# The first unit of a fused attention and gated-FFN kernel: pair 0 on the hardware queue, key maxima from PSUM, masks laid a pair ahead

## The chip, the cores and the metric

The kernel runs on one core of one Trainium2 chip. The metric is the device time in microseconds. The time before is the median of three runs, 265.78 us (265.74 to 267.43).

## The reference

Sparse attention with a window and block summaries, followed by a gated FFN with a gated residual. Cut to what matters:

```
B, H, S, D = 4, 8, 768, 64;  block, window = 32, 16
k_sum = k.reshape(B, H, nb, block, D).max(axis=3)       # maxima of 32 keys, nb = 24
v_sum = v.reshape(B, H, nb, block, D).mean(axis=3)
scores_l = scale * q @ k.T,  masked where |i - j| >= window
scores_s = scale * q @ k_sum.T + log(block)
a = softmax(concat(scores_l, scores_s))                 # over keys and block maxima together
attn = a @ concat(v, v_sum)
x = attn, heads side by side                            # (3072, 512)
ffn = (gelu(x @ w_gate) * (x @ w_val)) @ w_out          # d_ff = 1536
out = x + sigmoid(x @ w_res) * ffn
```

## The kernel before

The 3072 rows are eight units of 384 tokens (half a batch of 768 each). A unit is attention for eight heads, taken as four pairs of heads, and then the FFN: 12 steps `fo` over d_ff, residual gate, output matmul. From unit 1 on, the attention of the next unit is woven into the end of the unit before. Unit 0 has nothing before it: its attention is the head of the program, written out by hand, and the order on each engine is the order of the program text.

All loads of k, q, v and the weights are software DMAs that GpSimd issues and that cast f32 to bf16 on the way. In the head GpSimd issues, in this order: k of heads 0 to 3, q of heads 0 to 3 (the first 384 tokens only, tile `qa`), k of heads 4 to 7, q of heads 4 to 7, chunks 0 to 6 of v (with the selects that build the mask `maskt`, the bias `bias_t` and the mean matrix `bmean` between them), then six slices each of `w_gate` and `w_val`, q's second half of batch 0 (`qb`), `w_res`, `w_out`, and in unit 0's step 4 the rows of batch 1. At most eight software DMAs are open at once: each waits for the one eight places before.

For each pair, `k_step` turns k with 16 TensorE transposes into one PSUM tile `tp`; ScalarE (ACT) copies it into `kW`, whose 128 columns for each 64-token tile hold the tile's own 64 keys, 16 on either side (the halo, copied from the neighbours) and 24 block maxima. `k_rest` builds the maxima on VectorE (DVE) from `kW` (L206, L208), copies the halos (L210, L211) and spreads the maxima to all 12 tiles (L212). `q_step` does the same for q with one ACT copy (L216). `mask_step` lays -30000 outside the window into the score tile by a matmul with `nmask` (L279); `s_step` adds the scores (L296), and ACT takes the exponential to `P` (L305, or L302 twice when the two heads lie in two tiles). The text of the head turns pairs 0 and 1 first, then scores pair 0, turns pair 2, scores pair 1, turns pair 3, scores pairs 2 and 3.

The values `vext` need two copies from their own loads (`v_spread`, L266, L269). `vsum_sum` (L254) makes the block means with seven matmuls, one a chunk of v. `av_part` multiplies P with the window's values and with the block means (L328), `av_norm` divides (L336, L338), and `xt_step` turns the result (L347). `keep_warm` issues matmuls of zeros. The first FFN matmuls are `gv` at L360. PSUM has four tiles `mm`, one `s` of double size, one `ao` and one `t`.

SP's queue carries only the outputs and, from unit 2 on, transposing DMAs.

Of the kernel before, what the change touches and what calls it, by code (L numbers as in the profile page):

```python
# [8 lines left out]
F32 = mybir.dt.float32  # L9
BF16 = mybir.dt.bfloat16  # L10
AF = mybir.ActivationFunctionType
ALU = mybir.AluOpType
# [3 lines left out]
def kernel(  # L16
# [11 lines left out]
    nc = tc.nc  # L28
    B, H, S, D = q.shape
    assert (B, H, S, D) == (4, 8, 768, 64)  # L30
    BLK, WIN = 32, 16
    NB = S // BLK
# [5 lines left out]
    FO = DFF // 128  # L38
    QT = 64
# [63 lines left out]
    with tc.manual_schedule():  # L103
# [17 lines left out]
        def mask_consts():  # L121
            nc.vector.memset(maskt[:], 1.0)
            select(maskt[0:96], ALU.is_ge, 0.0, -1, -1, 1)
            select(maskt[0:96], ALU.is_ge, 0.0, 2 * WIN - 1, 1, -1)
            nc.vector.tensor_scalar(nmask[:], maskt[:], 30000.0, -30000.0, ALU.mult, ALU.add)

# [4 lines left out]
        nc.vector.memset(bmean[:], 1.0 / BLK)  # L131
        vext_consts(0)

        kt, qa, qb = token_tile(0, S, "k0"), token_tile(0, TU, "qa"), token_tile(TU, S, "qb")
        k_sb[0] = kt
        load_tokens(kt, k, 0, 0, S, 0, 4)
        select(ident[:], ALU.not_equal, 1.0, 0, -1, 1)
        load_tokens(qa, q, 0, 0, TU, 0, 4)
        load_tokens(kt, k, 0, 0, S, 4, 8)
        load_tokens(qa, q, 0, 0, TU, 4, 8)  # L140
        select(bias_t[96:128, :], ALU.is_ge, -30000.0, NB - 1, 0, -1)
        load_values(0, 0)
        mask_consts()
        kw_consts(0)
        load_values(0, 1)
        select(bmean[:], ALU.is_ge, 0.0, 32 * (NB + 94) - WIN, -32, 1)
        select(bmean[:], ALU.is_ge, 0.0, 31 + WIN - 32 * (NB + 94), 32, -1)
        for c in range(2, NC + 1):
            load_values(0, c)
        nc.vector.memset(vsum[0][96:128, :, D:D + 1], 1.0)  # L150
# [3 lines left out]
        for c in range(6):  # L154
            sl = slice(c * 256, (c + 1) * 256)
            nc.gpsimd.dma_start(out=w_gate[:, :, sl], in_=wg_src[:, :, sl])
            nc.gpsimd.dma_start(out=w_val[:, :, sl], in_=wv_src[:, :, sl])
        load_tokens(qb, q, 0, TU, S, 0, H)
# [55 lines left out]
        def q_step(src, b, lo, hi, hp, pool, tag):  # L214
            tp = turn_pair(src, hp, pool, tag)
            nc.scalar.copy(qT[b % 2][hp][:, lo:hi].rearrange("d (p j) -> d p j", j=tp.shape[2]), tp)  # L216
# [59 lines left out]
        def mask_step():  # L276
            s = ps_s.tile([128, 2, 512], F32, tag="s", name="s")
            for hh in range(2):
                nc.tensor.matmul(s[:, hh, 0:TU].rearrange("p (t q) -> p t q", t=HT), ident[:],  # L279
                                 nmask.unsqueeze(1).to_broadcast([128, HT, QT]),  # L280
                                 start=True, stop=False, skip_group_check=True)
            return s

        def s_step(u, hp, st, s=None, two=None, masked=True):
            b, half = u // 2, u % 2
            first = s is not None
            if two:
                s = [pool.tile([128, 512], F32, tag=tag, name="s1") for pool, tag in two]
            elif not first:
                s = ps_s.tile([128, 2, 512], F32, tag="s", name="s")  # L290
# [120 lines left out]
        def values_step(u, fo):  # L411

            b = u // 2 + 1
            first = 8
            if u in (2, 4) and first - 3 <= fo < first + 1:
                block_sums(vT[b], fo - first + 3)
            if u in (1, 2, 4) and fo >= first:
                nb = 1 if u == 1 else b
                i = fo - first
                if i == 0 and u == 1:  # L420
                    vs = vsum_sum(nb, *SS)
                    vsum_out(nb, vs, 0, H, nc.scalar.copy)
                if i == 0:
                    v_spread(nb, 0, HT // 2, 0)
                if i == 2 and u > 1:
                    vsum_turn(nb, *SS)
                if i == 1:
                    v_spread(nb, 0, HT // 2, 1)
                if i in (2, 3):
                    vsum_bc(nb, 2 * i - 4, 0, HT)  # L430
                    vsum_bc(nb, 2 * i - 3, 0, HT)
# [9 lines left out]
        wp = ps_o.tile([128, 512], F32, tag="ao", name="wp")  # L441
        keep_warm(13, wp)
        nc.scalar.activation(pre[:], bias_t[0:1, :], AF.Exp)
        for hp in range(2):
            k_step(0, hp, *MM)
            q_step(qa, 0, 0, TU, hp, *MM)
        s = mask_step()
        keep_warm(3, wp)
        s_step(0, 0, st, s)
        k_step(0, 2, *MM)  # L450
        q_step(qa, 0, 0, TU, 2, *MM)
        s = mask_step()
        s_step(0, 1, st, s)
        k_step(0, 3, *MM)
        q_step(qa, 0, 0, TU, 3, *MM)
        s = mask_step()
        s_step(0, 2, st, s)
        v_spread(0, 0, HT // 2, 0)
        v_spread(0, 0, HT // 2, 1)
        vs = vsum_sum(0, *MM, range(0, 3))  # L460
        keep_warm(2, wp)
        s = mask_step()
        s_step(0, 3, st, s)
        keep_warm(2, wp)
        for c in range(3, NC + 1):
            vsum_sum(0, *MM, range(c, c + 1), vs)
            keep_warm(2 if c < NC else 1, wp)
        vsum_out(0, vs, 0, 2, nc.vector.tensor_copy)
        vsum_out(0, vs, 2, 8, nc.scalar.copy)
        nc.scalar.activation(pre[:], bias_t[0:1, :], AF.Gelu)  # L470
        homes = (AO, TT, MM, MM)
        for p in (0, 2):
            for hp in (p, p + 1):
                av_part(0, hp, st, *homes[hp], blocks=False)
            for hp in (p, p + 1):
                av_part(0, hp, st, blocks=True)
                av_norm(hp, st)
        keep_warm(3)
# [7 lines left out]
        for u in range(NU):  # L486
# [9 lines left out]
            for fo in range(FO):  # L496
# [29 lines left out]
                if u == 0 and fo >= FO - 2:  # L526
                    for hp in range(2 * (fo - FO + 2), 2 * (fo - FO + 2) + 2):
                        q_step(qb, 0, TU, S, hp, *(TT if hp % 2 else AO))
# [95 lines left out]
```

The softmax here doesn't subtract the row's maximum and nothing guards it: scores larger than these inputs give would overflow.

## Time and profile before

| what | value |
|---|---|
| median of three runs | 265.78 us |
| profiled execution, its own time | 265.32 us |
| its span | 263.4 us |
| TensorE busy | 254.6 us, 97% of the span |
| VectorE, ScalarE, GpSimd busy | 174.0, 139.0, 93.5 us |
| granted TensorE clock | 1.00 in every stretch |
| first FFN matmul (gv) starts | 22.78 us |

The span runs from the first to the last instruction of the profiled execution; 1.9 us of its own time lie around it. Shares of busy time are averages over stages that differ: the first 25 us are a chain of loads, turns, scores and values, and the rest is a steady stream of matmuls. A line "L360" is line 360 of the kernel.

### The profile page before, as it was taken

Reading aid. Unit: us, or ns where it says so; the run is one execution under the profiler, and the core shown is the slowest. Engines: PE = TensorE matmul, PEld = TensorE weight load, DVE = VectorE, ACT = ScalarE, POOL = GpSimd, SP = SyncE. Lnnn points to the kernel's source line nnn. Section 1 sums busy time; section 2 is a strip of 40 time slices with the busy share of each in tenths; the row PEclk is TensorE's granted clock in tenths of the full one; section 3 lists DMA queues with packets and bytes.
Section 4 is the critical chain, followed back from the end, with each engine's and each line's share of the span. In section 5 each row is a group of like instructions: output and inputs, shape, how many; then the busy total and the mean of one; then the engine's idle time right before and its main releaser. Section 6 shows DMA issues by size and latency. Waiting matters only on the chain.

```text
span 263.4 us, 5865 instructions
## 1 busy us (share of the span) xinstructions
PE 254.6 (97%) x2324; PEld 143.9 (55%) x2324; DVE 174.0 (66%) x414; ACT 139.0 (53%) x240; POOL 93.5 (36%) x124
## 2 busy tenths in 40 slices
PE   6799999999999999999999999999999999999994
PEld 2546555566555555555545565556555665556543
DVE  3744863498476889877837899678738853574424
ACT  2845449657565536754365536653375537553310
POOL 7976533997999107998300000000000000000000
PEclk9999999999999999999999999999999999999999
DMA  5999999999999979999991466224001200020012
GB/s 82 171 172 197 197 206 189 147 177 176 118 117 127 201 126 110 158 173 181 144 48 44 115 119 103 46 82 100 2 1 42 80 0 2 36 86 1 2 40 80
DMA packets 109259, 27.64 MB, mean 105 GB/s; under 512 B 95408, under 2 KB 106288, under 8 KB 109232
## 3 DMA queue, kind: packets, MB, share of 16 engines
q0 software_dynamic: 86032, 16.26, 83.2%
q1 hardware_dynamic: 23200, 11.02, 18.0%
q8 instruction: 18, 0.29, 0.5%
q14 instruction: 9, 0.07, 0.1%
HBM read 32.51 MB, written 6.29 MB: 147 GB/s over the span
## 4 chain that ended last, share of the span: by engine, by line
PE 89%; POOL 3%; DMA 3%; DVE 2%; issue 1%; ACT 1%; POOLq 0%; DVEq 0%
PE f L394 24%; PE g L360 23%; PE vv L360 22%; PE r L378 8%; PE ao L328 4%; DMA vext<-in_v_dram 3%; PE s L296 2%; PE xp L347 2%; POOL vext L99 2%; PE tp L185 1%; PE vs L254 1%; DVE gvT L367 1%; PE gv L360 1%; PE wp L409 1%; POOL k L90 1%
## 5 line engine op out<-in xcount | busy, mean ns | idle before, releaser
L360 PE MATMUL g<-xT,w_gate 128*128 128x384 bf16 x380 | 77.8, 326 | 0.5 <-DVE gvT L367 0.5
L366 ACT ACTIVATE ge<-g 128x384 f32<-128x384 f32 x95 | 46.7, 492 | 59.5 <-PE g L360 30.3
L360 PE MATMUL vv<-xT,w_val 128*128 128x384 bf16 x380 | 77.8, 326 | 0.1
L367 DVE TENSOR_TENSOR gvT<-ge,vv 128x384 bf16<-128x384 f32 x95 | 51.9, 552 | 30.9 <-PE vv L360 27.6
L394 PE MATMUL f<-w_out,gvT 128*128 128x512 bf16 (+2 forms) x312 | 69.5, 363 | 0.0
L360 PEld LDWEIGHTS <-w_val 128*128 128x128 bf16 x384 | 37.5, 98 | 25.6 <-issue 1.0
L360 PEld LDWEIGHTS <-w_gate 128*128 128x128 bf16 x384 | 36.9, 98 | 25.1 <-issue 1.1
L394 PEld LDWEIGHTS <-gvT 128*128 128x128 bf16 x312 | 27.6, 98 | 25.6
L349 ACT COPY xT<-xp 128x384 bf16<-128x384 bf16 x32 | 15.1, 481 | 22.6 <-PE xp L347 22.6
L378 PE MATMUL r<-w_res,xT 128*128 128x512 bf16 x96 | 24.4, 380 | 0.0
L399 DVE SCALAR_TENSOR_TENSOR th<-th,f 128x512 f32<-128x512 f32 (+2 forms) x26 | 16.7, 642 | 11.4 <-PE f L394 8.5
L172 POOL DMA_DIRECT2D k_sb<-in_k_dram x24 | 20.1, 864 | 11.6 <-DMA w_out<-in_moe_w_out_dram 5.2
L99 POOL DMA_DIRECT2D vext<-in_v_dram x28 | 23.2, 866 | 0.9 <-PE g L360 0.6
L384 ACT ACTIVATE th<-r 128x512 f32<-128x512 f32 x24 | 14.2, 602 | 17.4 <-PE r L378 17.4
L313 DVE TENSOR_TENSOR P<-P,maskt 128x768 bf16<-128x768 bf16 x28 | 15.5, 557 | 10.3 <-ACT P L305 7.5
L172 POOL DMA_DIRECT2D q_sb<-in_q_dram x24 | 19.9, 862 | 0.0
L338 DVE TENSOR_TENSOR xn<-ao,rz 128x384 bf16<-128x384 f32 x32 | 17.8, 558 | 1.1
L305 ACT ACTIVATE P<-s,bias_t 128x768 bf16<-128x768 f32 x18 | 16.2, 903 | 3.1 <-PE s L296 2.9
L336 DVE RECIPROCAL rz<-ao 128x6 f32<-128x6 f32 x32 | 6.1, 190 | 17.4 <-PE ao L328 17.4
L401 DVE SCALAR_TENSOR_TENSOR o<-th,xn 128x512 f32<-128x512 f32 (+2 forms) x26 | 16.9, 651 | 0.9
L302 ACT ACTIVATE P<-s,bias_t 128x384 bf16<-128x384 f32 x28 | 14.6, 578 | 0.0
L172 POOL DMA_DIRECT2D v_sb<-in_v_dram x16 | 13.5, 874 | 1.2 <-DMA q_sb<-in_q_dram 0.7
(82 smaller groups left out, 218.4 us busy)
## 6 DMA issues: line engine op xcount, KB each, us to landing
out_dram<-o SPq DMA_DIRECT2D x23, 256.0 KB, 2.6
vext<-in_v_dram POOLq DMA_DIRECT2D x20, 128.0 KB, 6.6
k_sb<-in_k_dram POOLq DMA_DIRECT2D x24, 96.0 KB, 6.1
q_sb<-in_q_dram POOLq DMA_DIRECT2D x24, 96.0 KB, 4.4
w_gate<-in_moe_w_gate_dram POOLq DMA_DIRECT2D x6, 256.0 KB, 8.6
w_val<-in_moe_w_val_dram POOLq DMA_DIRECT2D x6, 256.0 KB, 8.8
w_out<-in_moe_w_out_dram POOLq DMA_DIRECT2D x3, 512.0 KB, 14.1
v_sb<-in_v_dram POOLq DMA_DIRECT2D x16, 96.0 KB, 5.0
```

Of the source, the lines that this page charges most:

```text
L99: nc.gpsimd.dma_start(out=dst, in_=v[b, :, lo:hi, :].rearrange("h p d -> p h d"))
L172: nc.gpsimd.dma_start(out=sb[b][:, h // 2, :, h % 2 * D:h % 2 * D + D], in_=src[b, h].rearrange("(c p) d -> p c d", c=NC))
L305: nc.scalar.activation(P.rearrange("p a t q -> p a (t q)"), s[:, :, 0:TU], AF.Exp, scale=scale, bias=bias_t[:])
L313: nc.vector.tensor_mul(Pf, Pf, maskt.unsqueeze(1).to_broadcast([128, 2 * HT, QT]))
L338: nc.vector.tensor_mul(xn, ao[:, :, :, 0:D], rz.to_broadcast([128, NSUB, 2, D]))
L360: nc.tensor.matmul(acc[:, 0:TU], w[:, ko, fs], st["xT"][:, ko, :], start=(ko == 0), stop=(ko == KO - 1))
L366: nc.scalar.activation(ge[:], g[:, 0:TU], AF.Gelu)
L367: nc.vector.tensor_mul(gvT[:, fo, :], ge[:], vv[:, 0:TU])
L378: nc.tensor.matmul(r[:], st["xT"][:, ko, ss], w_res[:, ko, :], start=(ko == 0), stop=(ko == KO - 1))
L394: nc.tensor.matmul(st["f", sub][:, 0:c1 - c0], gvT[:, fo, ss], w_out[:, fo, c0:c1], start=(fo == 0), stop=(fo == FO - 1))
L399: nc.vector.scalar_tensor_tensor(th, th, 1.0, f[:, 0:c1 - c0], ALU.add, ALU.mult)
L401: nc.vector.scalar_tensor_tensor(o[:, 0:c1 - c0], th, 0.5, st["xn"][:, sub, c0:c1], ALU.mult, ALU.add)
```

## The change

Pair 0 of k and q goes by SP's hardware queue as f32 into two tiles `kf` and `qf`; ACT casts `kf` into `kt` and VectorE casts `qf` into `qa`. GpSimd loads the other three pairs one by one. `k_first` replaces `k_step` in the head: same transposes and ACT copy, but the maxima are one VectorE reduce straight from the PSUM tile, and halos and maxima are laid only for the six tiles of unit 0. The other six follow in `k_later`, at steps 4 to 7 of unit 0's FFN. In the head q's copy is VectorE's. Each pair's masks are laid before the scores of the pair ahead of it, for pairs 1 and 3 into `ao` and `t`. The turns of a pair now stand behind the scores of the pair before. There are 12 warming matmuls in place of 30. The block means are split between the scores and the value parts. q's second half is loaded before the last slice of the gate weights and turned at step 9, all four pairs together, in place of steps 10 and 11. In unit 1 the block means and the spreads of the next batch's values move from steps 8 and 9 to steps 9 and 10.

```diff
+        kw_consts(0)
+        nc.vector.memset(vsum[0][96:128, :, D:D + 1], 1.0)
...
-        load_tokens(kt, k, 0, 0, S, 0, 4)
+        kf = qk.tile([PP, 2, 8 * D], F32, tag="k_sb", name="kf")
+        qf = qk.tile([PP, 2, 4 * D], F32, tag="q_sb", name="qf")
+        nc.sync.dma_start(out=kf[:], in_=k[0, 0:2].rearrange("h (p j) d -> p h (j d)", j=8))
+        nc.sync.dma_start(out=qf[:], in_=q[0, 0:2, 0:TU].rearrange("h (p j) d -> p h (j d)", j=4))
+        load_tokens(kt, k, 0, 0, S, 2, 4)
         select(ident[:], ALU.not_equal, 1.0, 0, -1, 1)
-        load_tokens(qa, q, 0, 0, TU, 0, 4)
-        load_tokens(kt, k, 0, 0, S, 4, 8)
-        load_tokens(qa, q, 0, 0, TU, 4, 8)
+        load_tokens(qa, q, 0, 0, TU, 2, 4)
+        for h in (4, 6):
+            load_tokens(kt, k, 0, 0, S, h, h + 2)
+            load_tokens(qa, q, 0, 0, TU, h, h + 2)
+        load_values(0, 0)
+        select(maskt[0:96], ALU.is_ge, 0.0, -1, -1, 1)
+        select(maskt[0:96], ALU.is_ge, 0.0, 2 * WIN - 1, 1, -1)
         select(bias_t[96:128, :], ALU.is_ge, -30000.0, NB - 1, 0, -1)
-        load_values(0, 0)
-        mask_consts()
-        kw_consts(0)
-        load_values(0, 1)
+        for c in range(1, NC + 1):
+            load_values(0, c)
         select(bmean[:], ALU.is_ge, 0.0, 32 * (NB + 94) - WIN, -32, 1)
         select(bmean[:], ALU.is_ge, 0.0, 31 + WIN - 32 * (NB + 94), 32, -1)
-        for c in range(2, NC + 1):
-            load_values(0, c)
-        nc.vector.memset(vsum[0][96:128, :, D:D + 1], 1.0)
...
         for c in range(6):
             sl = slice(c * 256, (c + 1) * 256)
+            if c == 5:
+                load_tokens(qb, q, 0, TU, S, 0, H)
...
-        load_tokens(qb, q, 0, TU, S, 0, H)
...
-        def q_step(src, b, lo, hi, hp, pool, tag):
+        def q_step(src, b, lo, hi, hp, pool, tag, copy=nc.scalar.copy):
...
+        def k_first(hp):
+            tp = ps_mm.tile([128, 8, PP], BF16, tag="mm", name="tp")
+            for j in range(8):
+                for hh in range(2):
+                    nc.tensor.transpose(tp[hh * 64:hh * 64 + 64, j, :], kt[:, 2 * hp + hh, j, :], ident[0:PP, 0:PP])
+            kw = kW[0][hp]
+            nc.scalar.copy(kw[:, :, OWN:OWN + QT].rearrange("d t (p j) -> d t p j", j=8),
+                           tp.rearrange("d j (t p) -> d t p j", t=NT))
+            return tp, kw
+
+        def k_first_rest(tp, kw):
+            ks = work.tile([128, NB], BF16, tag="ks", name="ks")
+            nc.vector.tensor_reduce(out=ks[:], in_=tp.rearrange("d j (n w) -> d n j w", w=4),
+                                    axis=mybir.AxisListType.XY, op=ALU.max)
+            nc.vector.tensor_copy(kw[:, 0:HT, BLK0:BLK0 + NB], ks.unsqueeze(1).to_broadcast([128, HT, NB]))
+            nc.vector.tensor_copy(kw[:, 1:HT, 0:WIN], kw[:, 0:HT - 1, OWN + QT - WIN:OWN + QT])
+            nc.vector.tensor_copy(kw[:, 0:HT, POST:POST + WIN], kw[:, 1:HT + 1, OWN:OWN + WIN])
+
+        def k_later(kw):
+            nc.vector.tensor_copy(kw[:, HT:NT, 0:WIN], kw[:, HT - 1:NT - 1, OWN + QT - WIN:OWN + QT])
+            nc.vector.tensor_copy(kw[:, HT:NT - 1, POST:POST + WIN], kw[:, HT + 1:NT, OWN:OWN + WIN])
+            nc.vector.tensor_copy(kw[:, HT:NT, BLK0:BLK0 + NB], kw[:, 0:HT, BLK0:BLK0 + NB])
...
-            first = 8
+            first = 9 if u == 1 else 8
...
-        wp = ps_o.tile([128, 512], F32, tag="ao", name="wp")
-        keep_warm(13, wp)
         nc.scalar.activation(pre[:], bias_t[0:1, :], AF.Exp)
-        for hp in range(2):
-            k_step(0, hp, *MM)
-            q_step(qa, 0, 0, TU, hp, *MM)
-        s = mask_step()
-        keep_warm(3, wp)
-        s_step(0, 0, st, s)
-        k_step(0, 2, *MM)
-        q_step(qa, 0, 0, TU, 2, *MM)
-        s = mask_step()
-        s_step(0, 1, st, s)
...
+        keep_warm(8)
+        nc.scalar.copy(kt[:, 0:2].rearrange("p h j d -> p h (j d)"), kf[:])
+        nc.vector.tensor_copy(qa[:, 0:2].rearrange("p h j d -> p h (j d)"), qf[:])
+
+        def first_pair(hp):
+            t = k_first(hp)
+            q_step(qa, 0, 0, TU, hp, *MM, nc.vector.tensor_copy)
+            k_first_rest(*t)
+
+        first_pair(0)
+        nc.vector.tensor_scalar(nmask[:], maskt[:], 30000.0, -30000.0, ALU.mult, ALU.add)
+        keep_warm(1)
+        masked = [mask_step(), mask_step((AO, TT))]
+        s_step(0, 0, st, masked[0])
+        first_pair(1)
+        masked.append(mask_step())
+        keep_warm(1)
+        s_step(0, 1, st, masked[1], True)
+        first_pair(2)
+        masked.append(mask_step((AO, TT)))
+        keep_warm(1)
+        s_step(0, 2, st, masked[2])
+        first_pair(3)
+        keep_warm(1)
+        vs = vsum_sum(0, *SS, range(0, 2))
+        s_step(0, 3, st, masked[3], True)
+        nc.scalar.activation(pre[:], bias_t[0:1, :], AF.Gelu)
         v_spread(0, 0, HT // 2, 0)
         v_spread(0, 0, HT // 2, 1)
-        vs = vsum_sum(0, *MM, range(0, 3))
...
+        vsum_sum(0, *SS, range(2, 4), vs)
+        homes = (MM, MM, AO, TT)
+        for hp in range(2):
+            av_part(0, hp, st, *homes[hp], blocks=False)
+        vsum_sum(0, *SS, range(4, 5), vs)
+        for hp in range(2, NP):
+            av_part(0, hp, st, *homes[hp], blocks=False)
+        vsum_sum(0, *SS, range(5, NC + 1), vs)
         vsum_out(0, vs, 0, 2, nc.vector.tensor_copy)
         vsum_out(0, vs, 2, 8, nc.scalar.copy)
...
+        for hp in range(NP):
+            av_part(0, hp, st, blocks=True)
+            av_norm(hp, st)
-        keep_warm(3)
...
-                if u == 0 and fo >= FO - 2:
-                    for hp in range(2 * (fo - FO + 2), 2 * (fo - FO + 2) + 2):
+                if u == 0 and 4 <= fo < 8:
+                    k_later(kW[0][fo - 4])
+                if u == 0 and fo == FO - 3:
+                    for hp in range(NP):
                         q_step(qb, 0, TU, S, hp, *(TT if hp % 2 else AO))
```

## The prediction

> **What bounds the kernel now.** I read four views in this order: the page's engine row, the chain that ended last over the first 50 us, the timeline of the first 25 us, and the waits and DMA issues. The page says that TensorE is busy nearly throughout:
>
> ```profile
> PE 254.6 (97%) x2324; PEld 143.9 (55%) x2324; DVE 174.0 (66%) x414; ACT 139.0 (53%) x240; POOL 93.5 (36%) x124
> ```
>
> So from the first FFN matmul on, a microsecond is won or lost only where TensorE waits. The change touches the head, before that matmul, and two spots of unit 0's FFN loop. The chain over the head (start us, us, what):
>
> ```profile
> 10.25 7.42 DMA vext<-in_v_dram
> ...
> 17.71 0.38 PE vs L254
> ...
> 19.22 2.07 PE ao L328 x96
> ...
> 22.78 0.48 PE gv L360 x2
> ```
>
> The head ends when the first FFN matmul (gv) starts, at 22.78, and what ends last there is the load of v: its sixth chunk lands at 17.67, then come block means, attention times values, norms and transposes. The scores are not on this chain. The timeline shows how they run:
>
> ```profile
> 6.98 0.80 ACT L199 COPY kW<-tp 128x768 bf16<-128x768 bf16 x1 [4.67 <-PE tp L192]
> ...
> 7.81 0.36 DVE L206 TENSOR_TENSOR km<-kW 128x384 bf16<-128x384 bf16 x1 [0.46 <-ACT kW L199]
> ...
> 8.20 0.55 DVE L208 TENSOR_REDUCE ks<-km 128x24 bf16<-128x384 bf16 x1
> ...
> 8.90 0.60 DVE L212 COPY kW<-ks 128x288 bf16<-128x288 bf16 x1
> ...
> 10.10 0.90 ACT L305 ACTIVATE P<-s,bias_t 128x768 bf16<-128x768 f32 x1 [0.73 <-PE s L296]
> ...
> 10.49 0.22 DVE L212 COPY kW<-ks 128x288 bf16<-128x288 bf16 x1
> 10.90 0.79 ACT L199 COPY kW<-tp 128x768 bf16<-128x768 bf16 x1
> ...
> 15.79 0.90 ACT L305 ACTIVATE P<-s,bias_t 128x768 bf16<-128x768 f32 x1 [0.86 <-PE s L296]
> ```
>
> The exponentials P of pairs 0 and 3 start at 10.10 and 15.79: three pairs in 5.69, 1.90 each. That is possible because k and q of pairs 0 and 1 are both turned before the first P, so that while P of one pair runs, the next pair's key columns are already built.
>
> **Step 1, pair 0 arrives earlier.** Its k (384 KB as f32) and q (192 KB) go out on SP's queue, which is empty until the first output:
>
> ```profile
> out_dram<-o SPq DMA_DIRECT2D x23, 256.0 KB, 2.6
> ...
> out_dram<-o SPq DMA_DIRECT2D x1, 128.0 KB, 1.7
> ```
>
> No f32 load on this queue is in the trace. From below, 384 KB is the 2.6 of 256 KB plus 128 KB at the 394 KB/us at which f32 is read when the software queue is full (197 GB/s of bf16 in the windows): 2.9. From above it goes on with the step from 128 to 256 KB, 0.9 per 128 KB: 3.5. Issue at about 0.85 (ACT's first instruction stands at 0.81) gives 3.8 to 4.35; I take 4.0. [...]
>
> The new ACT cast of 96x1024: ACT copies of 384 and 768 columns take 0.48 and 0.80, so 0.83 ns a column and 0.16 fixed, 1.01: ends 5.06. Sixteen transposes, 0.53, end 5.63; kW copy 0.80, ends 6.47 (before: 7.78). VectorE's reduce of 768 from PSUM replaces a max (0.36) and a reduce of 384 (0.55): between 0.80 (ACT's pass over the same 768 columns) and 1.1 (twice the reduce); I take 0.95, near the 0.91 it replaces. The built program has it wait for ACT's kW copy, as these two readers of one PSUM tile were ordered before:
>
> ```profile
> ACT vsum L259 <- DVE vsum L259: 2.5, 1, 2.5
> ```
>
> So taking the maxima from PSUM saves nothing. Three smaller copies at the spacing of 0.12 seen before: 0.48, ends 7.93; nmask 0.1; four mask matmuls 0.66 (0.16 apart before), two more than before ahead of the first scores; scores 0.35, hand-overs 0.2: P of pair 0 at 9.2. Short VectorE copies are sometimes held while GpSimd builds descriptors (0.60 against 0.22 for the same L212 copy in the rows above); with 0.1 for that, **9.3**, bounds 8.4 (load 0.6 earlier, reduce 0.80, nothing held) to 10.0.
>
> **Step 2, what happens between the pairs.** This is what decides. In the changed program the order on ACT is kW0, P0, kW1, P1, kW2, P2, kW3, P3, and on TensorE the transposes of a pair stand behind the scores of the pair before. The look-ahead of one pair is gone: behind P of one pair wait kW of the next, then VectorE's maxima and copies, then TensorE's scores, then the next P. One round: P start to kW end 1.59 (10.10 to 10.90 + 0.79 in the rows), hand-over 0.03, reduce 0.95, copies 0.48, hand-over 0.15, scores 0.35, hand-over 0.06: 3.61. After pair 1, whose masks lie in two tiles and whose P is two instructions (two took 1.04 at 43.24), 3.74. q's copies, moved to VectorE, lie beside P and cost nothing; on ACT they would add 0.49 a round. The masks laid ahead also lie under P; behind it they would cost 0.5. Three rounds are 10.96; with 0.15 each for held VectorE copies 11.4 (bounds 10.5, with a reduce of 0.80 and nothing held, to 12.2). P of pair 3 starts at **20.7** instead of 15.79.
>
> **Step 3, from the last P to gv.** VectorE ends pair 3's key columns 0.56 before its P, then does both v_spread copies, 0.70 each (they stood at 15.15 and 15.88, under the wait for v): 21.6, and the first attention matmul waits for them. Four window parts at 0.27 and a chunk of block means 0.16, 22.85; the last two chunks 0.35; vsum to VectorE 0.30, 23.55; to ACT 0.47, 24.0; three block parts 0.8, 24.8; transpose and ACT's copy 0.7: gv at 25.55, or P + 4.85 (bounds 4.5 to 5.2). The three warming matmuls behind this stage (0.75 in the chain) are gone, which is counted here.
>
> Is v there? It is ahead of this. The software queue loses 288 KB of 1920, 1.5 us at its 190 KB/us. GpSimd issues six smaller loads for four ahead of v: +0.6 to +1.2; and the bmean selects (0.71) move behind v. The issues of v keep 0.88 each, the last full one near 10.6, landing (4.3 to 7.7 after issue in the batch-1 loads) at 15 to 18.3, under 21.6 all the same.
>
> So gv moves from 22.78 to **25.55, +2.8** (bounds +0.6: 8.4 + 10.5 + 4.5; +4.6: 10.0 + 12.2 + 5.2).
>
> **Step 4, unit 0's FFN.** The second half of the key columns (12 copies, 0.4 a pair at the spacing above) now stands in VectorE's queue at steps 4 to 7. At step 4 it follows the constants of batch 1, behind which TensorE already waited for a product at 34.65: +0.45 there (bounds 0 and 1.6, all four). From step 5 on VectorE has 0.56 + 0.4 of 1.30, covered. Turning q's second half at step 9 puts four pairs in a row on two tiles: the third waits for ACT's first copy, about 0.5 lost; in exchange the two waits of 0.4 to 0.5 at 40.3 to 41.2, where scores waited for these tiles, go: +0.1 (bounds -0.4 and +0.5). qb's load passes two of 256 KB, 2.6 us earlier than its 35.5, and slice 5 falls 2.0 behind while the queue is 1.5 ahead: it had landed at 33.6 for 36.6, so it costs nothing; uncovered 0.5. The moved value step of unit 1 leaves VectorE 0.75 behind at step 10; the scores and residual matmuls (some 4 us) before its product is needed hide it, else 0.75.
>
> **Sum:** +2.8 + 0.45 + 0.1 = +3.3. The profiled execution took 265.32 (span 263.4 and 1.9 around it), so 268.6; the median of the runs is 0.46 above that execution, so **269.0** against 265.78.
>
> **Rivals.**
> (a) *The same chain, but short.* k lands by 3.4, nothing holds VectorE, step 4 is hidden: +0.8 to +2.6, 266.6 to 268.4, within 1%. For it: most 0.22 copies were not held. Against it: GpSimd issues DMAs through the whole head.
> (b) *TensorE's clock falls.* The opening matmuls show a slow start: weight loads follow each other at 0.43, then five in 0.96; the granted clock reads 1.00 in both stretches, so that view will not tell.
>
> ```profile
> 3.80 0.15 PEld L409 LDWEIGHTS <-warm 128*128 128x128 bf16 x1 [0.28 <-issue]
> ...
> 4.17 0.96 PEld L409 LDWEIGHTS <-warm 128*128 128x128 bf16 x5 [0.22 <-issue]
> ```
>
> Before, TensorE never idles over 0.8 in the head; now it works some 1.7 of each 3.8, with about 2.1 idle in one piece and 18 of 30 warming matmuls gone. If it falls back, about 3 us of dense work on the way to gv and behind it take twice as long: +1.5 to +3, 270.5 to 272. [...]
> (c) *v still decides, and it is faster.* With v landed at 15.2 and gv 5.1 behind as now, less the 0.75 of warming, gv starts at 19.6: -3.2 + 0.5, 263.1. It begins to win when P of pair 3 starts before 17.9 (22.78 - 4.85), a round of 2.87 from 9.3. For it: v is the bound today and gets lighter. Against it: ACT alone holds 1.6 of each round, and reduce, copies and scores follow in a row.
> (d) *The maxima run beside ACT's copy after all.* 0.8 off each of three rounds and off pair 0: P of pair 3 at 17.5, gv at 22.35, 265.9. The built wait speaks against it.
>
> **How the numbers follow.** My forecast (268.4 to 270.5) 0.48; (a) 0.27; (b) 0.17; (c) 0.04; (d) 0.04. A measurement of this kernel can tell about 1%, 2.7 us. Slower by more than 1%: the forecast and (b), 0.65; within: (a) and (d), 0.31; faster: (c), 0.04. The range 266.8 to 271.4 takes in nearly all of (a) and half of (b), and leaves out some 0.17.
>
> **What would show it.** Right: P of pairs 0 to 3 some 3.7 apart, kW of a pair directly behind P of the one before; gv near 25.5; the chain through the head on ACT kW, DVE ks and kW, PE s, with no DMA of v. Wrong: starts of P less than 2.9 apart; the reduce starting before ACT's copy ends; gv before 22.8. Step 1 is wrong if the cast starts outside 3.4 to 4.6; step 4 if step 5's product does not come late; (b) shows in the spacing of the attention and first FFN matmuls.

## The result, and the profile after

The changed kernel took 275.56 us (median of 4 runs, 273.9 to 275.68) against 266.06 for the kernel before: a ratio of 1.033, 95% interval 1.028 to 1.039. It is slower by 9.5 us, where the forecast was 3.3. The profiled execution took 273.9, with a span of 272.2 against 263.4.

The page of the changed kernel, its engine row and its row of TensorE's granted clock (tenths of full speed in 40 slices of the span):

```profile
PE 256.0 (94%) x2282; PEld 145.4 (53%) x2306; DVE 176.8 (65%) x427; ACT 138.9 (51%) x239; POOL 94.3 (35%) x126
...
PEclk9765699999999999999999999999999999999999
```

TensorE is busy a little longer than before (256.0 against 254.6) with fewer instructions: some of them ran slower. The clock row, which was all nines before, falls in slices 2 to 5, about 7 to 34 us.

The timeline of the head (start us, us, engine, line):

```profile
6.76 0.96 DVE L232 TENSOR_REDUCE ks<-tp 128x24 bf16<-128x768 bf16 x1
...
8.32 1.28 PE L308 MATMUL s<-nmask,ident 128*128 128x384 bf16 x4 [1.94 <-DVE nmask L481]
...
10.14 0.90 ACT L334 ACTIVATE P<-s,bias_t 128x768 bf16<-128x768 f32 x1 [3.41 <-PE s L325]
10.94 0.79 ACT L226 COPY kW<-tp 128x768 bf16<-128x768 bf16 x1
...
13.72 1.05 ACT L331 ACTIVATE P<-s,bias_t 128x384 bf16<-128x384 f32 x2 [1.99 <-PE s L325]
...
17.55 0.90 ACT L334 ACTIVATE P<-s,bias_t 128x768 bf16<-128x768 f32 x1 [2.09 <-PE s L325]
...
21.21 1.05 ACT L331 ACTIVATE P<-s,bias_t 128x384 bf16<-128x384 f32 x2 [2.06 <-PE s L325]
...
28.58 0.50 PE L376 MATMUL xp<-ident,xn 128*128 128x128 bf16 x3 [1.10 <-DVE xn L367]
...
29.65 0.48 PE L389 MATMUL gv<-xT,w_gate 128*128 128x384 bf16 x1
```

The P's stand 3.58, 3.83 and 3.66 apart, each with kW of the next pair directly behind it; the chain that ended last runs over kf's load, ScalarE's kW copies, VectorE's reduces and copies and the scores, with no transfer of v. So far it is the chain of the forecast. Two things are not: masks that should take 0.66 took 1.28, and from P of pair 3 to the first FFN product gv it is 8.44 us instead of 4.85.

The stretches of 5 us show why (stretch, its length, then busy us and count of PE, PEld, DVE, ACT and POOL, granted clock, DMA share, GB/s):

```profile
5.00:10.00 5.00, 2.70 (x43) 1.41 (x45) 2.41 (x7) 1.10 (x2) 4.80 (x9) 0.85 1.46 172
10.00:15.00 5.00, 3.38 (x67) 2.34 (x66) 2.52 (x6) 2.87 (x5) 4.88 (x8) 0.81 2.20 134
15.00:20.00 5.00, 3.02 (x40) 1.64 (x39) 2.68 (x6) 2.05 (x3) 5.00 (x8) 0.53 1.31 164
20.00:25.00 5.00, 4.32 (x66) 2.28 (x65) 1.91 (x6) 2.54 (x4) 2.68 (x4) 0.50 1.41 187
25.00:30.00 5.00, 3.32 (x57) 2.34 (x57) 3.03 (x9) 1.14 (x3) 1.81 (x3) 0.50 1.45 197
30.00:35.00 5.00, 5.00 (x29) 2.86 (x28) 0.57 (x2) 2.28 (x6) 2.81 (x4) 0.76 1.42 199
```

In stretches of 1 us the clock is at half from 8.5 to 11.9, full again until 15.3, and at half from there to 32.4 us: in the whole stage behind the last P, and in the first 2.7 us of the FFN. The product of step 2 starts 8.2 us later than before (34.00 against 25.79), gv 6.9 later; the 1.3 between them is dense work at half rate (products 0.32 apart up to 32.17, 0.16 from 32.62 on). The span is 8.8 longer.

### The profile page after: what moved, and what is told of

Same layout as the page of the kernel before. It is cut to its first block, busy times and chain, and to the rows that moved or that the text cites. A ratio compares the mean times of both kernels' runs of the same rounds, so it can differ in the third digit from the quotient of the medians.

```text
span 272.2 us, 5827 instructions
## 1 busy us (share of the span) xinstructions
PE 256.0 (94%) x2282; PEld 145.4 (53%) x2306; DVE 176.8 (65%) x427; ACT 138.9 (51%) x239; POOL 94.3 (35%) x126
## 3 DMA queue, kind: packets, MB, share of 16 engines
HBM read 32.51 MB, written 6.29 MB: 143 GB/s over the span
## 4 chain that ended last, share of the span: by engine, by line
PE 85%; DVE 6%; DMA 4%; ACT 2%; issue 1%; DVEq 0%; ACTq 0%
PE f L423 23%; PE g L389 21%; PE vv L389 20%; PE r L407 8%; PE ao L357 3%; PE s L325 3%; DMA kW<-k_sb 3%; PE xp L376 2%; PE vs L280 2%; DVE ks L232 1%; DMA kf<-in_k_dram 1%; PE tp L186 1%; DVE xn L367 1%; ACT kW L226 1%; PE gv L389 1%
## 5 line engine op out<-in xcount | busy, mean ns | idle before, releaser
L423 PE MATMUL f<-w_out,gvT 128*128 128x512 bf16 (+2 forms) x298 | 68.6, 362 | 0.7
L407 PE MATMUL r<-w_res,xT 128*128 128x512 bf16 x88 | 23.6, 380 | 0.6 <-issue 0.3
L428 DVE SCALAR_TENSOR_TENSOR th<-th,f 128x512 f32<-128x512 f32 (+2 forms) x26 | 16.7, 641 | 11.4 <-PE f L423 8.5
L331 ACT ACTIVATE P<-s,bias_t 128x384 bf16<-128x384 f32 x32 | 16.7, 578 | 4.1 <-PE s L325 4.1
L334 ACT ACTIVATE P<-s,bias_t 128x768 bf16<-128x768 f32 x16 | 14.4, 901 | 7.1 <-PE s L325 7.0
L357 PEld LDWEIGHTS <-P 128*64 128x64 bf16 (+2 forms) x432 | 9.7, 120 | 8.2 <-issue 7.6
## 6 DMA issues: line engine op xcount, KB each, us to landing
out_dram<-o SPq DMA_DIRECT2D x23, 256.0 KB, 2.0
w_gate<-in_moe_w_gate_dram POOLq DMA_DIRECT2D x6, 256.0 KB, 8.6
w_val<-in_moe_w_val_dram POOLq DMA_DIRECT2D x6, 256.0 KB, 9.9
```

The source lines that it names most:

```text
L331: nc.scalar.activation(P[:, hh].rearrange("p t q -> p (t q)"), s[hh][:, 0:TU], AF.Exp, scale=scale, bias=bias_t[:])
L357: nc.tensor.matmul(ao[64 * e:64 * e + 64, sub, hh, :], P[rows, hh, t, :], rhs, start=blocks is None or (not blocks and sub == 0 and hh == ...
L407: nc.tensor.matmul(r[:], st["xT"][:, ko, ss], w_res[:, ko, :], start=(ko == 0), stop=(ko == KO - 1))
L423: nc.tensor.matmul(st["f", sub][:, 0:c1 - c0], gvT[:, fo, ss], w_out[:, fo, c0:c1], start=(fo == 0), stop=(fo == FO - 1))
L428: nc.vector.scalar_tensor_tensor(th, th, 1.0, f[:, 0:c1 - c0], ALU.add, ALU.mult)
```

## The experiments

Theory A: the clock takes the larger part of the loss, the lost look-ahead the rest. Theory B: the look-ahead is everything, the clock only a record. Theory C, added when the traces were compared: the first transposes of x wait for the wrong buffer. The diffs are against the changed kernel unless another is named.

### The clock: warming matmuls in the gaps (e1)

```diff
-        keep_warm(1)
+        keep_warm(8)
         masked = [mask_step(), mask_step((AO, TT))]
...
-        keep_warm(1)
+        keep_warm(7)
         s_step(0, 1, st, masked[1], True)
...
         homes = (MM, MM, AO, TT)
+        keep_warm(3)
...
             av_norm(hp, st)
+        keep_warm(3)
```

The gaps behind pairs 2 and 3 have seven as well.

> The changed kernel with warming matmuls of zeros (8, 7, 7 and 7, and 3 on either side of the value parts) in the gaps where TensorE waited; nothing else moved. Theory A (the clock gate took most of the loss, about 6 of 9 us, the lost look-ahead the rest): the granted clock stays at 1.00, the exponentials P of the four pairs still start about 3.6 apart, gv starts near 26 instead of 29.65, total 269 to 270. Rival B (the lost look-ahead is the whole cost, the slow clock only a record of the idling): gv stays near 29, total 274 to 276.

Measured: 272.24, ratio 1.022 (1.018 to 1.025), 3.3 less than the change, between the two theories; gv at 28.00 instead of 29.65. The clock was 1.00 from 5 to 25 us, but 0.51 in the next stretch:

```profile
25.00:30.00 5.00, 4.53 (x48) 2.65 (x43) 2.41 (x7) 1.17 (x3) 2.62 (x4) 0.51 1.45 197
```

So B's 274 to 276 is out, and A half shown: the clock fell again, and in the middle of work. These are 1-us stretches, and the block parts (P times the block means) in which it fell; the row's bracket is the longest idle time of TensorE from 21.63 to 25.04:

```profile
24.00:25.00 1.00, 0.64 (x29) 0.52 (x30) 0.50 (x3) 0.47 (x1) 0.42 (x2) 1.00 1.46 198
25.00:26.00 1.00, 0.72 (x31) 0.71 (x26) 0.97 (x3) 0.00 (x0) 0.44 (x2) 0.54 1.45 205
...
24.23 1.49 PE L357 MATMUL ao<-vsum,P 32*64 32x65 bf16 x48 [0.39 <-DVE vsum L285]
```

From 21.63 to 25.04 TensorE was busy for 2.89 of 3.41 us, with no transpose among it: attention matmuls of 65 columns, and 0.65 us of block means.

### The look-ahead back, without and with warming (e2, e3)

```diff
         masked = [mask_step(), mask_step((AO, TT))]
-        s_step(0, 0, st, masked[0])
         first_pair(1)
-        masked.append(mask_step())
+        s_step(0, 0, st, masked[0])
         keep_warm(1)
-        s_step(0, 1, st, masked[1], True)
         first_pair(2)
+        masked.append(mask_step())
+        s_step(0, 1, st, masked[1], True)
...
```

> The changed kernel with the turns of pairs 1, 2 and 3 put before the scores of the pair ahead again; the warming matmuls stay as in the changed kernel (one a pair). Theory A: P of pair 3 starts near 16 to 17 instead of 21.2, but the clock still falls in the gap ahead of the first masks near 8, so the values and the first FFN matmuls run at half clock: gv near 24, total 268 to 271. Rival B: gv near 21.5, total 264 to 266.

Measured: 269.96, ratio 1.015 (1.012 to 1.017). P's 11.42, 13.43, 15.21, 17.23: 1.9 apart, as before the change. Yet gv started only at 24.42, 7.2 behind the last P, with the clock at 0.75 from 20 to 25 us and 0.57 in the next stretch, and with a wait that has nothing to do with either:

```profile
23.36 0.50 PE L376 MATMUL xp<-ident,xn 128*128 128x128 bf16 x3 [1.38 <-DVE xn L367]
```

e3 adds 4, 2, 3, 3, 3 warming matmuls in the gaps and three each ahead of the value parts and of x's transposes.

> Both: turns a pair ahead and the gaps filled with warming matmuls. Theory A: clock 1.00 throughout, P of pair 3 near 16.5, then v (landed near 17.4) or the spreads decide, gv near 21.5 to 22.5: 264.5 to 266, level with the kernel before or a little faster. Rival B: no better than the run with the turns alone.

Measured: 268.46 (266.48 to 270.77, 10 runs), ratio 1.008 (1.005 to 1.012). Short of what A gives; the runs differ by over 4 us, which left something open (see e13 and e14).

### Does a slow clock alone cost time? (e4)

The kernel before, without the 17 warming matmuls that follow the first 13.

> The kernel before without the 17 warming matmuls behind the opening 13 (3, 2, 2, 7 and 3 taken out), nothing else. Theory A: the clock falls to 0.5 somewhere between 8 and 20 and the values and first FFN matmuls run at half rate: 268 to 272. Rival B (only one gap longer than the 2 to 3 us now seen can make the clock fall; the kernel before has none over 1.5): the clock stays at 1.00, and without the 0.75 of the last three it is 265 to 266.

Measured: 266.38, ratio 0.999 (0.996 to 1.002). Both theories' numbers missed. The clock did fall, from 11.5 to 18.3:

```profile
10.00:15.00 5.00, 3.84 (x71) 2.32 (x64) 2.47 (x9) 3.52 (x5) 4.42 (x7) 0.65 3.25 148
15.00:20.00 5.00, 5.00 (x71) 2.23 (x70) 2.97 (x8) 2.57 (x5) 3.28 (x6) 0.67 1.82 176
20.00:25.00 5.00, 4.52 (x97) 3.27 (x92) 2.73 (x8) 3.53 (x7) 3.25 (x5) 1.00 1.45 197
```

It was back before the last stage. P of pair 3 came at 18.30 instead of 15.79, and yet gv at 22.50 instead of 22.78, since 17 warming matmuls fewer stood on the way. The right comparison is e12 below, which leaves out only four of the same matmuls and keeps the clock: P of pair 3 at 16.22, gv at 22.11. So of the 2.1 us by which the slow clock held the last scores, 0.4 reached gv; most of the rest lay in the 2.8 us that e12 spends behind its last scores on block means and the warming between them. It was not free: in e4 the chain to gv runs over the slow matmuls,

```profile
3.86 7.89 DMA qa<-in_q_dram
...
15.80 1.39 PE vs L254 x3
...
18.26 1.13 PE vs L254 x4
```

and no longer over v's load.

### The buffers of the first transposes (e5), and with warming (e6)

```diff
-            xt_step(0, hp, st, *(TT if hp % 2 else AO), nc.scalar.copy)
+            xt_step(0, hp, st, *(MM if hp < 2 else TT if hp % 2 else AO), nc.scalar.copy)
```

The changed kernel gives the accumulators of pairs 2 and 3 the buffers `ao` and `t` (`homes = (MM, MM, AO, TT)`; before `(AO, TT, MM, MM)`), and the first transposes of x write to the same two: they wait until pairs 2 and 3 are normalised.

> The changed kernel with one edit: the first two transposes of x go into mm tiles, since the tiles ao and t now hold the value parts of pairs 2 and 3 and are free only after the third and fourth norm. Theory C (this wait, which the prediction did not have, is a term of its own): the first transposes start at the end of the block parts, 1.0 to 1.5 earlier than at 28.58, gv near 28.3, total 273.8 to 274.8. Rival: the norms pace the transposes anyway (0.70 a pair), so 275 to 276.

Measured: 273.98, ratio 1.029 (1.025 to 1.033): 1.6 less than the change. With four runs of each the intervals of the two ratios overlap, so the size is uncertain; that the wait is gone shows in the trace, where the transposes follow the block parts directly:

```profile
26.85 1.71 PE L357 MATMUL ao<-vsum,P 32*64 32x65 bf16 x48 [0.39 <-DVE vsum L285]
...
28.49 0.98 PE L376 MATMUL xp<-ident,xn 128*128 128x128 bf16 x6
```

gv came at 29.56 although this execution's last P, at 22.17, came a microsecond later than the change's: 7.39 behind it instead of 8.44.

e6 is e1 with this, and three more warming matmuls ahead of the block sums' copies.

> The first experiment (gaps filled with warming matmuls) with that edit and three more warming matmuls ahead of the block parts, so that the clock stays up to the FFN. Theory A and C together: the clock is 1.00 through the head, what is left is the lost look-ahead alone: P of pair 3 near 20.5, gv near 25.5, total 268.5 to 269.5, which is what the prediction made without the clock. Rival B: 271 or more.

Measured: 270.76, ratio 1.015 (1.010 to 1.021), between the two forecasts, clock 1.00 in every stretch. With e5 this prices the clock: 273.98 - 270.76 = 3.2, less what the warming itself costs. The two traces have it by place: P of pair 0 0.2 (11.18 against 10.99), three rounds 0.3 (10.99 against 10.70), last P to gv 1.1 (7.39 against 6.30), gv to the product of step 2 2.1 (5.09 against 3.01). That is 3.7 up to there; the two executions as a whole differ by 2.9.

### Warming only from the last gap on (e9)

e6 with one warming matmul in each of the first three gaps, as the changed kernel has.

> The kernel e6 (changed kernel, first two transposed tiles of x in other buffers, warming matmuls throughout) with only one warming matmul in each of the first three gaps, as the changed kernel has; the warming from pair 3's gap on stays (7, 3, 3, 3). Theory A': a round between two P is ScalarE and VectorE work (kW copy, reduce, copies), so a slow clock costs nothing there and all of its price is paid behind the last P; and without eight warming matmuls ahead of the first masks P of pair 0 comes earlier (10.1 to 11 instead of 11.0). Median 269.5 to 271, that is e6's 270.76 or a little less; the clock at 0.5 to 0.9 between 8 and 20 us and at 1.00 from 22 us on; three rounds 10.6 to 11.1. Rival: each round pays for its transposes, masks and scores at half rate, 0.5 a round and 0.3 at the opening: three rounds of 12.2 and a median of 272.3 or more.

Measured: 272.68, ratio 1.023 (1.019 to 1.028): worse than e6 by 1.9. The time is the rival's, the place is neither's:

```profile
19.14 3.17 PE L438 MATMUL wp<-warm 128*128 128x512 bf16 x7
...
22.85 0.35 PE L325 MATMUL s<-qT,kW 64*128 64x64 bf16 x12
```

The first two rounds were 3.80 and 3.98 (e6: 3.51 and 3.68), 0.3 each for the slow clock (0.77 from 10 to 15 us, 0.57 from 15 to 20); then the seven warming matmuls, themselves slow, held the scores of pair 3, whose key columns were complete at 21.14, and the last round took 5.08. From P to gv it was 6.29, as in e6. These seven began with the clock down and took 3.17; the same seven in e6, at 1.00, took 1.69.

### Look-ahead from pair 1 on (e8), and with late warming (e11)

e8 is e6 with pair 2 turned before the scores of pair 1 and pair 3 before those of pair 2.

> Both repairs and the tile edit on the changed kernel: pair 0 scored as soon as it is there, the turns of pairs 2 and 3 ahead of the scores of pairs 1 and 2, gaps filled. Theories A and C: clock 1.00, P of pairs 0 and 3 near 9.5 and 17, gv near 22, total 264.8 to 266; rival B: 267 or more.

Measured: 268.39, ratio 1.007 (1.005 to 1.010): 2.4 below e6, but in B's range and not in A's and C's. The clock was 1.00 in every stretch; what missed was P of pair 0, at 11.15 and not 9.5, behind eight warming matmuls that took 3.60. P of pair 3 at 19.43, gv at 25.72: again 6.29 behind.

e11 is e2 with e5's buffers, three warming matmuls ahead of the value parts and of the block sums' copies, and the second half of the key columns one step later.

> The changed kernel with the look-ahead back (turns of a pair ahead of the scores of the pair before, as in e2), the first two transposed tiles of x in other buffers, three warming matmuls ahead of the value parts and three ahead of the block sums, and the second half of the key columns at steps 5 to 8 instead of 4 to 7. By theory (look-ahead, clock behind the last P and the tile wait are the whole loss): P of pair 3 near 17.2 as in e2, gv 6.2 behind it at 23.4, the product of step 5 no later than the shift of the others: 265.8 to 267.2, ratio within 0.5% of the kernel before. Rival (the norms, v or the value copies hold the stage, as e3's gv at 25.55 with P at 18.32 suggests): gv at 24.5 or later and a median of 267.7 or more.

Measured: 268.91 (266.87 to 272.35, 12 runs), ratio 1.008 (1.005 to 1.011). The rival's number, but not its mechanism: without warming in the gaps the clock was 0.50 from 10 to 20 us in the profile, P of pair 3 came at 19.41, and gv 7.0 behind it.

### Maxima beside ScalarE's copy (e10)

e6 with k turned a second time into a tile of its own, from which VectorE takes the maxima ahead of q's copy. It makes rival (d) true.

> The kernel e6 with k of each pair transposed twice, into two tiles: ScalarE copies one, VectorE takes the maxima from the other at once, ahead of q's copy. This makes the fourth rival of the prediction true (the maxima run beside ScalarE's copy). If the round is the chain kW copy, reduce, copies, scores, as its steps have it: P start to reduce end about 1.3, q copy to 1.85, copies to 2.35, scores and hand-overs 0.5: rounds of 2.85 instead of 3.57, P of pair 3 2.1 to 2.5 earlier (19.2 to 19.6), gv at 25.5 to 26 and a median of 268.2 to 268.8 (e6: 270.76). If something else sets the end of the stage (v, the value copies), P comes earlier but gv stays near 28 and the median near 270.5. If the two passes over PSUM hold each other up, rounds stay above 3.3 and the median above 270.

Measured: 271.72, ratio 1.019 (1.016 to 1.023): no gain. Reduce and copy do run side by side, at 0.96 and 0.79 as in the changed kernel:

```profile
12.44 0.96 DVE L233 TENSOR_REDUCE ks<-t 128x24 bf16<-128x768 bf16 x1 [3.25 <-PE t L231]
...
12.50 0.79 ACT L226 COPY kW<-tp 128x768 bf16<-128x768 bf16 x1
```

But rounds shortened only to 3.30, 3.26 and 3.30: the reduce starts 0.74 behind P, when the second set of transposes is done, and q's copy then stands between it and the key columns. In the second and third round the scores also start 0.34 and 0.42 behind the finished key columns, behind e10's own warming and block means. The three rounds gained 0.8 together, and pair 0 lost 0.7 to the added transposes ahead of the warming.

### The opening, and everything undone but the loads (e13, e14)

Of the ten profiles with eight opening matmuls, up to e11, five turned pair 0's k in 0.53 us and five in 0.85. e13 is e6 with thirteen opening matmuls, and 4, 5, 5, 5 in the gaps. e14 is e3 with thirteen, e5's buffers, and three more ahead of the block sums' copies.

> The kernel e6 with thirteen opening warming matmuls, as the kernel before has, instead of eight, and 4, 5, 5, 5 in the gaps behind the four pairs instead of 8, 7, 7, 7. Of ten profiles with eight opening matmuls five turned pair 0's k at full rate (0.53 us) and five at half rate (0.85); in e6 it was half, and its eight warming matmuls then took 3.27 ahead of the masks, so P of pair 0 started at 10.99. Theory D (the cut opening is a cost of its own, and the rest of e6's loss is the lost look-ahead at full clock): transposes at 0.53 in the profile, P of pair 0 near 10.0, rounds of 3.55, P of pair 3 at 20.6 to 20.9, gv at 26.6 to 27.2, a median of 269.0 to 270.0 and a spread under 1.5. Rival (the opening doesn't matter, the two groups of e6's times come from elsewhere): P of pair 0 still at 10.8 or later and a median of 270.3 to 271.5.

> The kernel e3 (turns of a pair ahead of the scores of the pair before, warming in the gaps) with thirteen opening warming matmuls instead of eight, the first two transposed tiles of x in other buffers, and three warming matmuls ahead of the block sums: every part of the change that the runs found to cost time undone, and its loads, its maxima from PSUM, its order of the value parts and its moved steps kept. By theory D with the others: P of pair 0 at 10.8, P of pair 3 at 17 to 17.8, gv at 23.2 to 24, a median of 266.2 to 267.2. Rival (the stage behind the last P is itself 1.3 longer than before at any clock): gv at 24.3 or later and a median of 267.4 to 268.5.

Measured: e13 271.28, ratio 1.018 (1.016 to 1.021); e14 267.36, ratio 1.004 (1.002 to 1.007).

```profile
1.26 5.18 PE L438 MATMUL wp<-warm 128*128 128x512 bf16 x13 [1.26 <-DVE warm L121]
...
6.38 0.53 PE L224 MATMUL tp<-ident,k 96*64 96x96 bf16 x16
```

In e13 the transposes ran at full rate and the spread was 0.95, as theory D had it, but the median is the rival's: thirteen matmuls last until 6.4, and pair 0's k, cast by 5.37, waits for them. P of pair 0 started at 10.49, so the opening is a trade and no gain.

e14 landed just above D's 267.2, and less than 0.5% above the kernel before:

```profile
17.52 1.05 ACT L331 ACTIVATE P<-s,bias_t 128x384 bf16<-128x384 f32 x2 [0.96 <-PE s L325]
...
23.80 0.32 PE L389 MATMUL gv<-xT,w_gate 128*128 128x384 bf16 x1 [0.16 <-ACT xT L378]
```

e13 and e14 differ in the look-ahead alone (and a few warming matmuls): 271.28 - 267.36 = 3.9, and gv 27.82 against 23.80, 4.0.

### The hardware-queue load alone (e7), and a leaner kernel before (e12)

e7 is the kernel before with pair 0 of k and q by SP's queue and cast; nothing else.

> The kernel before with the hardware-queue load of pair 0 alone (kf, qf, the two casts, GpSimd's first two loads halved). If the load of v is the bound and the software queue gets 1.5 lighter: P of pair 0 near 9, v's sixth chunk near 16.3 instead of 17.67, gv near 21.5, total 264.3 to 265. Rival: v's landing is set by GpSimd's issue times, which do not move: gv at 22.5 or later, total 265.5 to 266.5.

Measured: 266.16, ratio 0.999 (0.997 to 1.002). P of pair 0 at 9.65 instead of 10.10, gv at 23.41 instead of 22.78 with the clock at 0.66 from 10 to 15 us, where the masks took 0.82 instead of 0.50; that is part of the delay. The chain to gv begins with the software queue's load of the other pairs' q, which lands at 10.98; pair 0 is not on it, so its 0.45 buys nothing here. What it is worth with the clock kept was not tried.

e12, against the kernel before, leaves out the last four warming matmuls:

```diff
-            keep_warm(2 if c < NC else 1, wp)
+            if c < NC:
+                keep_warm(2, wp)
...
-        keep_warm(3)
```

> The kernel before without the last four warming matmuls (one behind the last chunk of block means, three ahead of the first transposes of x): the first attention matmul no longer stands behind 0.37 of warming, nor the first transpose of x behind 0.75. If these matmuls stand on the chain that sets the end, as the chain of waits shows, gv starts 0.6 to 0.9 earlier than 22.78 and the median is 265.2 to 265.7. Rival 1 (the clock falls in the gaps left, the first product at half rate): 266.2 to 268. Rival 2 (norms of the second pair of pairs or the weights set the FFN's pace anyway): gv earlier, step 2's product where it was, 266.0 to 266.3.

Measured: 265.57 (12 runs), ratio 0.997 (0.995 to 0.999): faster than both kernels, as forecast, if by 0.3%.

```profile
21.20 0.52 PE L347 MATMUL xp<-ident,xn 128*128 128x128 bf16 x6
...
22.11 0.32 PE L360 MATMUL gv<-xT,w_gate 128*128 128x384 bf16 x1 [0.39 <-ACT xT L349]
```

gv started 0.67 earlier, and the clock stayed at 1.00, so these four warming matmuls were not needed to keep it. In the profiled execution (265.45) the 0.6 stands until 128 us, and a wait of 1.3 for a product of gvT in a later unit, 0.5 in the profile of before, takes it back; the medians have it.

## Why the prediction was right in direction and short by six microseconds

The direction and the chain through the head came out; the size did not. By the runs the 9.5 us are:

| part | from which runs | us |
|---|---|---|
| wait for the accumulators' buffers | 275.56 to 273.98 (e5) | 1.6 |
| slow clock, less the price of the warming | 273.98 to 270.76 (e6) | 3.2 |
| lost look-ahead | e13 to e14 | 3.9 |
| what stays | e14 over its 266.02 | 1.3 |

They add to 10.0; the half over 9.5 is e13's distance from e6, within the intervals.

**Step 1 held, with a price at the end.** kf landed at 4.23 (4.0 said), its cast took 1.04 (1.01), kW's copy ended at 6.73 (6.47), the reduce took 0.96 (0.95) and waited for ScalarE's copy as said. Then masks at half rate made 1.28 of 0.66, and P of pair 0 came at 10.14 (9.3, bound 10.0).

**Step 2 was right.** Three rounds took 11.07, forecast 11.4; P of pair 3 21.21, forecast 20.7: pair 0 was 0.8 late and the rounds 0.3 shorter. The time allowed for held VectorE copies, 0.1 and three times 0.15, did not show: the three copies of a pair took 0.49, 0.45, 0.38 and 0.38 (0.48 said before that allowance), beside GpSimd's issues, and no run shows that these issues are what makes a copy long. e14 against e13 shows that the lost look-ahead costs 3.9 when the clock is full. At full clock and with the buffers right, e6 took 270.76, 1.8 over the forecast and inside its range.

**Step 3 failed: P of pair 3 to gv, 4.85 forecast, 8.44 measured.** Three terms were missed.

- The clock, 1.1 of it, and 1.3 more in the FFN behind gv (2.1 in e5, whose clock recovered later: 0.60 from 30 to 35 us, against 0.76). The fall stood as rival (b), put at 1.5 to 3; e5 and e6 measure 3.2. The fault was the chance, 0.17: I took the longest gap, 2.1 by my sum and 1.94 in the trace, as the whole case, and that the clock would outlast it was not shown by the trace of before, where TensorE stands idle for at most 0.78 between two matmuls of the head. The stretches of 1 us show that the clock fell right behind that gap:

```profile
7.00:8.00 1.00, 0.00 (x0) 0.00 (x0) 0.96 (x4) 0.00 (x0) 0.88 (x2) 1.00 1.20 172
8.00:9.00 1.00, 0.68 (x3) 0.35 (x3) 0.27 (x4) 0.00 (x0) 1.00 (x2) 0.76 1.61 180
9.00:10.00 1.00, 1.00 (x16) 0.38 (x16) 0.00 (x0) 0.00 (x0) 1.00 (x3) 0.50 1.90 132
```

What I had not counted is how little work TensorE had before the masks: between the end of the opening at 4.86 and the masks at 8.32 stand 0.39 us of plain matmul and 0.69 of transposes in 3.46. That does not explain every fall: in e1 the clock fell after 2.89 us of plain matmul in 3.41, with no transpose and no gap over 0.39. What the clock counts stays open.

- The buffer wait, 1.05 in the traces (8.44 against e5's 7.39) and 1.6 in the medians with the clock's share in it. The forecast counted "three block parts 0.8" and then the transpose, and did not ask in which PSUM tiles the accumulators now lay. The line that shows it is the transposes of x at 28.58, before which TensorE stood idle for 1.10 until a norm ended. It was the third pair's, at 28.53, whose buffer they needed; pair 0's own `xn` had been ready since 27.14.
- The stage itself. At full clock with the buffers right it took 6.30 in e6 and e13, 6.29 in e8 and e9 and 6.28 in e14, against 4.85. Some of that is those kernels' own warming, as two pairs of rows of e6 show (the sums in VectorE's hands at 25.18, the block parts at 25.53; `xn` of pair 0 at 26.74, its transposes at 27.09):

```profile
24.88 0.30 DVE L285 CAST vsum<-vs 32x128 bf16<-32x128 f32 x1 [2.25 <-PE vs L280]
...
25.53 0.97 PE L357 MATMUL ao<-vsum,P 32*64 32x65 bf16 x48
...
26.18 0.56 DVE L367 TENSOR_TENSOR xn<-ao,rz 128x384 bf16<-128x384 f32 x1
...
27.09 0.73 PE L376 MATMUL xp<-ident,xn 128*128 128x128 bf16 x6
```

In the changed kernel, without warming there, such hand-overs take 0.05, so this is about 0.6. I had also counted three block parts, 0.8, and no norm; from the start of the block parts to the end of pair 0's norm it took 1.21, and value parts and block means took 2.0 instead of 1.6. Without their warming the stage would take some 5.7, an estimate from these rows; no run has it at full clock without warming. The bounds of 4.5 to 5.2 were too narrow either way.

**Step 4 was right.** The product that stood at 34.65, behind the constants of batch 1, is at 43.00: 8.35 later, where the one ahead of it was 8.06 later, and the one behind it is 8.45 later (before, then after):

```profile
33.90 0.81 PE L360 MATMUL g<-xT,w_gate 128*128 128x384 bf16 x4
34.65 0.81 PE L360 MATMUL vv<-xT,w_val 128*128 128x384 bf16 x4
...
41.96 0.81 PE L389 MATMUL g<-xT,w_gate 128*128 128x384 bf16 x4
43.00 0.81 PE L389 MATMUL vv<-xT,w_val 128*128 128x384 bf16 x4 [0.23 <-DVE gvT L396]
```

So the key columns cost 0.4 (0.45 said), and the turns of q's second half nothing (0.1 said): the first residual matmul comes 8.47 later.

**The rivals.** (a) and (c) fell with the rounds: none was under 3.5. v's chain was not the bound, as argued; e7 shows that an earlier pair 0 moves nothing while other loads set the end. (The mark of 17.9 in (c) is where gv would stand as before; by its own gv of 19.6, v would decide only with P of pair 3 before 14.75.) (d) was mis-sized: e10 puts the reduce beside the copy and gains 0.3 a round, since the transposes, q's copy and its warming come between. (b) was real, and it did not replace the forecast but added to it: two rivals that go the same way are not alternatives, and the range should have reached to their sum, 269.0 + 3 = 272, before the missed terms.

Of the 1.3 in e14, 1.0 is there at gv, and still 1.0 at the product that stood at 33.90; behind the key columns it is 1.4. The 1.0 is about what e14's own warming takes in three places: its value parts start 0.45 behind the value copies, its block parts 0.35 behind their sums, x's transposes 0.36 behind `xn`, where the changed kernel, without warming there, has 0.09, 0.05 and 0.05. This is read from the traces; no run leaves that warming out with the clock kept, so it stays an estimate that the rest of the change costs little beyond the key columns. Why single runs of e3 differ by 4.3 us, and of e11 by 5.5, stays open.

## What to carry to other kernels

Ask of every stretch that a change thins out on TensorE how much large plain matmul work the last few microseconds hold (0.39 us in 3.46 ahead of the fall here), and not only how long the longest gap is (1.94); look at the granted clock, since no rule that these runs offer foretells every fall. Price the slow clock over everything dense behind it that lies on the chain; where there is slack, as in e4, little of it arrives (0.4 of 2.1). When an order changes, follow each buffer to its next user, since a new home for one tile is a new wait for another. Cutting a look-ahead trades one pair's latency for a full round trip per pair (3.9 us between e13 and e14), and loads that come earlier do not buy it back unless the load was on the chain (e7: P of pair 0 earlier by 0.45, gv not).

## What was not expected of the hardware

- The clock fell after a gap of 1.94 us in the changed kernel, and in e4 with no gap over 1.04. Ahead of the first stand 0.39 us of plain matmul in the 3.46 from 4.86 to 8.32, ahead of the second 0.85 in the 3.2 from 8.32 to 11.5; the rest is transposes and idle time. In e1 it fell with no gap over 0.39 and no transposes, after 2.89 us of mostly small attention matmuls in 3.41 (21.63 to 25.04).
- Behind eight opening matmuls, which took 3.46 to 3.60 us, the transposes of pair 0's k took 0.53 in five of ten profiles and 0.85 in five, while the granted clock read 1.00 from 5 to 10 us in all five of the slow ones. Behind thirteen (4.37 to 5.18 us) they took 0.53 in all six profiles. So the granted clock shows the later falls, but not the slow rate of the opening.
- In e10 VectorE and ScalarE read two tiles of PSUM at the same time, in 0.96 and 0.79, as long as in the changed kernel.
- 384 KB of f32 on SP's queue took 3.4 us from issue to landing in the changed kernel, 3.6 in e6 and 3.7 in e2.
